# Writing the fp32 matmuls of a transform as four with 32 weight columns each

## The chip, the cores and the metric

The kernel runs on one core of one Trainium2 chip. The metric is the device time of one execution in microseconds (us). A core has five engines that run their own instruction lists side by side: TensorE (PE, with its weight loads PEld), VectorE (DVE), ScalarE (ACT), GpSimd (POOL) and SyncE (SP), which here issues most of the DMA transfers.

## What is computed

A two-dimensional Fourier transform of 2 x 3008 x 256 numbers, of which the real part is kept, and on its rows two feed-forward blocks:

```python
def _attn_ref(x):
    X = np.fft.fft(x, axis=1)
    X = np.fft.fft(X, axis=2)
    return X.real.astype(np.float32)

def _moe_ref(x, w_in, w_out):
    h = x @ w_in
    g = h * (1.0 / (1.0 + np.exp(-h)))
    return (g @ w_out).astype(np.float32)

def _moe2_ref(x, w_in, w_out):
    h = x @ w_in
    relu6 = np.clip(h + 3.0, 0.0, 6.0)
    g = h * relu6 / 6.0
    return (g @ w_out).astype(np.float32)
```

6016 rows pass through both blocks, with w_in of 256 x 2048 and w_out of 2048 x 256.

## The kernel before

The transform stands at the beginning, and the two blocks, which are most of the time, behind it. The sequence of 3008 is split as 47 x 64, and the transform has three steps on TensorE, all in fp32.

**First step.** x arrives in twelve chunks (`XCH`; seven for the first batch, five for the second, of one to four slots). `load_x` issues a chunk's DMAs; `fold` adds and subtracts its parts on VectorE (L339, L343, L344); `step1` multiplies the folded parts (128 weight columns each) with the table `t1_sb`, 96 columns, and ScalarE copies the result into `out1` (L370). The first of the two matmul rows of a chunk needs L343, the second L344. There are four big x buffers, so `load_x(i + 4)` stands behind `step1(i)`: the ninth chunk waits for the matmuls of the fifth, the tenth for those of the sixth, the twelfth for the eighth's. The SP queue issues the x loads in that order, then the first raw weights (L110).

**Second and third step.** `steps23(g)` runs for twelve groups g: it evacuates the group before last from PSUM into `eo` (ScalarE), multiplies `out1` with `t2_sb` (L393, 129 columns, and L394, 127), adds a term while copying to `o2` (ScalarE up to g = 7, then VectorE at L401), and multiplies the `o2` of the group before with `t3_sb` (L411, 128 columns). The first groups alternate with the last chunks of the first step.

**Fillers.** `busy` (L351) puts matmuls of a zero tile `nil` between the first chunks.

**psl.** `step1_last` (L379) has matmuls of another form, eight with 32 weight columns each, written to the four quarters of the 128 output partitions; 12 columns stream through.

**Behind it.** VectorE decodes the first block's weights, which come as 64-bit words, in the order in which the code calls `advance`: its first operations stand right behind the last fold. `split` makes a high and a low part of `eo` in a shorter format (`xhi` on ScalarE, `xlo` at L190 on VectorE). The first product of a block is `win1` (L303 to L305): three matmuls, high with high, low with high, high with low. It needs the decoded weights, `xhi` and `xlo`. Within each engine the order is that of the code.

An fp32 matmul leaves two records in the trace, each with a weight load: fp32 goes through the array in two passes.

Of the kernel before, what the change touches and what calls it, by code (L numbers as in the profile page):

```python
# [49 lines left out]
FF, P = 2048, 128  # L50
# [33 lines left out]
def body(tc, xh, x128, t1, t2, t3, w1, w128, w2, out):  # L84
    nc = tc.nc
    V, A, T, G = nc.vector, nc.scalar, nc.tensor, nc.gpsimd
# [225 lines left out]
    nil = fft.tile([P, P], F32, name="nil")  # L312
    w128_raw = fft.tile([P, NF, 2], U32, name="w128_raw")
    t1_sb = fft.tile([P, 6 * 104], F32, name="t1_sb")
    t2_sb = fft.tile([P, 272], F32, name="t2_sb")
# [19 lines left out]
    def fold(i):  # L335
# [8 lines left out]
            V.tensor_tensor(out=x[:, :, 384:512], in0=x[:, :, 0:128], in1=x[:, :, 128:256], op=ALU.subtract)  # L344
        return y

    def busy(times):

        ps = psA.tile([P, 512], F32, name="psw", tag="s3")
        for _ in range(times):  # L350
            T.matmul(ps[:, 0:128], nil, nil, start=True, stop=True)  # L351

    def step1(i, x):
        n, c, k = XCH[i]
        for h in range(2):
            ps = psX.tile([P, XB, 96], F32, name="ps1", tag=f"s{h}")
            src = x[:, :, 256 + 128 * h : 384 + 128 * h]
            if SLOTS[c] == 0:
                T.matmul(ps[:, 0, :], src[:, 0], t1_sb[:, 288 + 96 * h : 384 + 96 * h], start=True, stop=False)
                T.matmul(ps[:, 0, 0:48], src[:, 1], t1_sb[:, 480 + 48 * h : 528 + 48 * h], start=False, stop=True)  # L360
                k, j = 1, 0
            else:
                whole = UNFOLDED.get(i, 0)
                for m in range(whole):
                    T.matmul(ps[:, m, :], x[:, m, 0:128], t1_sb[:, 96 * h : 96 * h + 96], start=True, stop=False)
                    T.matmul(ps[:, m, :], x[:, m, 128:256], t1_sb[:, 192 * h : 192 * h + 96], start=False, stop=True)
                for m in range(whole, k):
                    T.matmul(ps[:, m, :], src[:, m], t1_sb[:, 96 * h : 96 * h + 96], start=True, stop=True)  # L368
                j = SLOTS[c]
            A.activation(  # L370
                out1[n][:, h, :, :, j : j + k], ps[:, :k, :].rearrange("p n (s q) -> p q s n", s=2), AF.Copy
            )
# [12 lines left out]

    def step2(g):
        n, t = divmod(g, 6)
        ps = psA.tile([P, 2, 256], F32, name="ps2", tag="s2")
        o2 = fft.tile([P, 2, 256], F32, name="o2", tag="o2", bufs=3)
        for i in range(2):  # L390
            q = 4 * (2 * t + i)
            e, o = (out1[n][:, h, q : q + 4].rearrange("p q s j -> p (q s j)") for h in range(2))
            T.matmul(ps[:, i, 0:129], e, t2_sb[:, 0:129], start=True, stop=True)  # L393
            T.matmul(ps[:, i, 129:256], o, t2_sb[:, 129:256], start=True, stop=True)  # L394

        x128 = xr[:, n, 2 * t : 2 * t + 2]
        if g < 8:
            for i in range(2):
                A.activation(o2[:, i, 0:129], ps[:, i, 0:129], AF.Identity, bias=x128[:, i : i + 1])
        else:  # L400
            V.tensor_tensor(  # L401
                out=o2[:, :, 0:129], in0=ps[:, :, 0:129], in1=x128.unsqueeze(2).to_broadcast([P, 2, 129]), op=ALU.add
            )
        A.activation(o2[:, :, 129:256], ps[:, :, 129:256], AF.Copy)
        return o2

    def step3(o2):
        ps = psA.tile([P, 2, 256], F32, name="ps3", tag="s3")
        for h in range(2):
            for i in range(2):  # L410
                T.matmul(  # L411
                    ps[:, h, 128 * i : 128 * i + 128], o2[:, i, 128 * h : 128 * h + 128], t3_sb,
                    start=True, stop=True,
                )
        return ps

    def evacuate(g, ps):
        n, t = divmod(g, 6)
        c = HALFB * n
        if t == 0:  # L420
            A.activation(eo[:, :, c : c + SELF], ps[:, :, 0:SELF], AF.Identity, scale=sign)
            A.activation(eo[:, :, c + SELF : c + SELF + 192], ps[:, :, 64:256], AF.Identity, scale=sign)
            return c + SELF + 192
        c += SELF - 64 + 256 * t
        A.activation(eo[:, :, c : c + 256], ps, AF.Identity, scale=sign)
        return c + 256
# [20 lines left out]
    o2, full, done = {}, {}, 0  # L447
    folded = fold(0)
    i = g = 0
    busy(8)  # L450

    def step1_next():

        nonlocal folded, i
        x = folded
        if i + 1 < nx:
            folded = fold(i + 1)
        step1(i, x)
        if 3 <= i < nx - 4:
            load_x(i + 4, nc.sync, nc.sync)  # L460
        if i + 4 == nx - 1:
            load_raw(1, w1, 0)
        i += 1
        if i == 1:
            nc.sync.dma_start(t2_sb[:, 0:257], t2)
            nc.sync.dma_start(t3_sb, t3)
            nc.sync.dma_start(xl, x128)
        if i < 3:
            busy(3 - i)
        if i == 4:  # L470
            nc.sync.dma_start(w128_raw, w128)
        if i == 5:
            G.tensor_tensor(out=xl[:, 0], in0=xl[:, 0], in1=xl[:, 1], op=ALU.add)
        if i == 7:
            step1_last()
        if i == nx - 4:
            load_raw(1, w1, 1)
            advance(steps, 1)

    def steps23(g):  # L480
        nonlocal done
        if 0 <= g - 2 < 12:
            done = evacuate(g - 2, full.pop(g - 2))
        if g < 12:
            o2[g] = step2(g)
        if 0 <= g - 1 < 12:
            full[g - 1] = step3(o2.pop(g - 1))

    while XCH[i][0] == 0:
        step1_next()  # L490
    while i < nx:
        steps23(g)
        g += 1
        step1_next()
        if i == nx - 2:
            begin(1, 0)
        elif i == nx - 1:
            advance(steps, 2600)
# [89 lines left out]
    while g < 14:  # L588
        if g < 12:
            steps23(g)  # L590
        if g in (7, 10):
            xs[(g - 6) // 3] = split_eo((g - 6) // 3, (g - 6) // 3)
        if g >= 11 and g - 11 < EARLY:
            win1_end(*units[g - 11])
        if g >= 10 and g - 10 < EARLY + AHEAD:
            win1(*units[g - 10])
        if g in (11, 12):
            steps23(g + 1)
            if g == 12:
                idle = psA.tile([P, 512], F32, name="psi", tag="s2")  # L600
            parts(*units[g - 11])
        if g >= 12:
            for _ in range(FILL):
                T.matmul(idle[:, 0:128], nil, nil, start=True, stop=True)
        if g in (9, 11):
            do_later()
        advance(steps, 1700 if g < 8 else (1400, 700, 1400, 0)[g - 10] if g > 9 else 1400)
        g += 1
# [140 lines left out]
    for i in range(n1):  # L749
# [13 lines left out]
        while saves:  # L763
            dst, src = saves.pop(0)
# [110 lines left out]
    for e, (k, f) in enumerate(units2):  # L875
# [30 lines left out]
        while late:  # L906
            dst, src, to = late.pop(0)
# [181 lines left out]
```

## Time and profile before

| | |
|---|---|
| median of 3 runs | 916.25 us (916.05 to 916.52) |
| the profiled execution, its own time | 916.08 us |
| its span | 914.0 us |
| TensorE busy | 908.0 us, 99% of the span |
| VectorE, ScalarE, GpSimd busy | 73%, 71%, 58% |
| last fp32 matmul ahead of the first product | about 44 us |

The span is the time from the first to the last instruction of the profiled execution. Busy shares are means over stages with different limits; for a change in the first 44 us the windows there matter. A wait is told with what ended it. Matmuls are pipelined and their ends are modelled, so their starts say more than their durations.

### The profile page before, as it was taken

Reading aid. Unit: us, or ns where it says so; the run is one execution under the profiler, and the core shown is the slowest. Engines: PE = TensorE matmul, PEld = TensorE weight load, DVE = VectorE, ACT = ScalarE, POOL = GpSimd, SP = SyncE. Lnnn points to the kernel's source line nnn. Section 1 sums busy time; section 2 is a strip of 40 time slices with the busy share of each in tenths; the row PEclk is TensorE's granted clock in tenths of the full one; section 3 lists DMA queues with packets and bytes.
Section 4 is the critical chain, followed back from the end, with each engine's and each line's share of the span. In section 5 each row is a group of like instructions: output and inputs, shape, how many; then the busy total and the mean of one; then the engine's idle time right before and its main releaser. Section 6 shows DMA issues by size and latency. Waiting matters only on the chain.

```text
span 914.0 us, 12150 instructions
## 1 busy us (share of the span) xinstructions
PE 908.0 (99%) x4286; PEld 774.4 (85%) x4286; DVE 664.1 (73%) x907; ACT 649.6 (71%) x1144; POOL 528.3 (58%) x391
## 2 busy tenths in 40 slices
PE   9999999999999999999999999999999999999998
PEld 8988888888888888888878888888888888888886
DVE  7989999989999999994664565565555555555544
ACT  4878777665766666677876677766776777677665
POOL 2065656655565656554675567755765675576553
PEclk9999999999999999999999999999999999999999
DMA  8564344034272726596330002020020002001001
GB/s 319 194 220 159 136 148 140 9 138 139 96 211 87 214 107 164 176 359 201 135 79 13 1 1 91 0 91 1 1 91 0 1 1 90 1 1 46 1 1 45
DMA packets 29768, 89.29 MB, mean 98 GB/s; under 512 B 2886, under 2 KB 16460, under 8 KB 27180
## 3 DMA queue, kind: packets, MB, share of 16 engines
q1 hardware_dynamic: 27692, 81.83, 25.5%
q0 software_dynamic: 1632, 6.16, 3.6%
q8 instruction: 33, 0.54, 0.2%
q10 hardware_dynamic: 384, 0.54, 0.2%
q14 instruction: 27, 0.22, 0.1%
HBM read 52.31 MB, written 36.20 MB: 97 GB/s over the span
## 4 chain that ended last, share of the span: by engine, by line
PE 98%; DVE 1%; DMA 0%; ACT 0%; issue 0%; SPq 0%
PE y L305 18%; PE y L303 18%; PE y L304 18%; PE ab L303 5%; PE ab L304 5%; PE ab L305 5%; PE pa L303 3%; PE pa L305 3%; PE pa L304 3%; PE pb L303 2%; PE pb L304 2%; PE pb L305 2%; PE ps L368 1%; PE ps L411 1%; PE pd L304 1%; PE pc L303 1%
## 5 line engine op out<-in xcount | busy, mean ns | idle before, releaser
L806 POOL TENSOR_TENSOR glo<-h,ghi 128x500 fp32r<-128x500 f32 (+1 forms) x191 | 247.0, 1306 | 180.9 <-ACT ghi L803 176.7
L624 POOL TENSOR_TENSOR glo<-h,ghi 128x500 fp32r<-128x500 f32 (+1 forms) x137 | 212.6, 1564 | 188.3 <-ACT h L582 176.1
L303 PE MATMUL y<-ghi,whi 128*128 128x500 f32 (+1 forms) x768 | 294.3, 383 | 0.0
L304 PE MATMUL y<-glo,whi 128*128 128x500 f32 (+1 forms) x768 | 294.3, 383 | 0.0
L305 PE MATMUL y<-ghi,wlo 128*128 128x500 f32 (+1 forms) x768 | 294.3, 383 | 0.0
L305 PEld LDWEIGHTS y<-ghi,wlo 128*128 128x128 f32 x768 | 144.2, 188 | 25.7
L303 PEld LDWEIGHTS y<-ghi,whi 128*128 128x128 f32 x768 | 144.2, 188 | 25.6
L304 PEld LDWEIGHTS y<-glo,whi 128*128 128x128 f32 x768 | 144.2, 188 | 25.6
L803 ACT ACTIVATE ghi<-h 128x500 fp32r<-128x500 f32 (+1 forms) x192 | 118.1, 625 | 48.3 <-DVE h L798 46.2
L581 ACT ACTIVATE ghi<-ab 128x500 fp32r<-128x500 f32 (+1 forms) x96 | 56.4, 588 | 85.3 <-DVE h L572 83.5
L798 DVE SCALAR_TENSOR_TENSOR h<-h,pc 128x500 f32<-128x500 f32 (+1 forms) x96 | 65.0, 677 | 71.2 <-ACT h L795 71.2
L928 DVE TENSOR_TENSOR pc<-u,pb 128x500 f32<-128x500 f32 (+1 forms) x48 | 32.9, 686 | 105.3 <-ACT u L864 105.3
L795 ACT ACTIVATE h<-pc,consts 128x500 f32<-128x500 f32 (+1 forms) x96 | 64.7, 674 | 40.1 <-DVE pc L928 38.2
L864 ACT ACTIVATE u<-pa 128x500 f32<-128x500 f32 (+1 forms) x96 | 56.7, 591 | 46.6 <-PE pa L305 43.4
L303 PE MATMUL ab<-xhi,whi 128*128 128x500 f32 (+1 forms) x192 | 74.2, 386 | 0.2 <-DVE st L561 0.2
L304 PE MATMUL ab<-xlo,whi 128*128 128x500 f32 (+1 forms) x192 | 73.8, 384 | 0.0
L305 PE MATMUL ab<-xhi,wlo 128*128 128x500 f32 (+1 forms) x192 | 73.6, 383 | 0.0
L561 DVE SCALAR_TENSOR_TENSOR st<-eb,w_sb,ab 128x500 f32<-128x500 f32 (+1 forms) x92 | 66.9, 727 | 6.4 <-PE ab L305 6.3
L572 DVE SCALAR_TENSOR_TENSOR h<-st,ab 128x500 f32<-128x500 f32 (+1 forms) x92 | 61.2, 665 | 6.1 <-PE ab L305 6.1
L795 ACT ACTIVATE h<-pd,consts 128x500 f32<-128x500 f32 (+1 forms) x96 | 64.8, 675 | 0.6 <-DVE pd L940 0.6
L798 DVE SCALAR_TENSOR_TENSOR h<-h,pd 128x500 f32<-128x500 f32 (+1 forms) x96 | 64.3, 670 | 1.2 <-ACT h L795 1.2
L582 ACT ACTIVATE h<-h 128x500 f32<-128x500 f32 (+1 forms) x96 | 60.0, 625 | 3.1
(165 smaller groups left out, 1574.6 us busy)
## 6 DMA issues: line engine op xcount, KB each, us to landing
raw<-in_w SPq DMA_DIRECT2D x16, 1024.0 KB, 6.9
y_d<-st SPq DMA_DIRECT2D x5, 1000.0 KB, 5.1
y_d<-st POOLq DMA_DIRECT2D x5, 1000.0 KB, 8.1
u<-y_d SPq DMA_DIRECT2D x5, 1000.0 KB, 5.4
out<-st SPq DMA_DIRECT2D x19, 250.0 KB, 2.2
w2h_d<-h SPq DMA_DIRECT2D x8, 512.0 KB, 2.6
w2l_d<-t SPq DMA_DIRECT2D x8, 512.0 KB, 3.3
whi<-w2h_d SPq DMA_DIRECT2D x8, 512.0 KB, 5.8
```

What stands on the lines that cost most here:

```text
L303: T.matmul(o, wh, xhi, start=first, stop=False, **group)
L304: T.matmul(o, wh, xlo, start=False, stop=False, **group)
L305: T.matmul(o, wl, xhi, start=False, stop=last, **group)
L561: V.scalar_tensor_tensor(out=z[:, :n], in0=eb[:, :n], scalar=w128_sb[:, f : f + 1], in1=ab[:, :n], op0=ALU.mult, op1=ALU.add)
L572: V.scalar_tensor_tensor(out=h[:, 0, :n], in0=z[:, :n], scalar=2.0, in1=ab[:, :n], op0=ALU.mult, op1=ALU.subtract)
L582: A.activation(h[:, s, :n], src, AF.Silu)
L624: eng.tensor_tensor(out=glo[:, s, :n], in0=h[:, s, :n], in1=ghi[:, s, :n], op=ALU.subtract)
L795: A.activation(h[:, i, :n], c[:, :n], AF.Relu, bias=three)
L798: V.scalar_tensor_tensor(out=h[:, i, :n], in0=h[:, i, :n], scalar=6.0, in1=c[:, :n], op0=ALU.min, op1=ALU.mult)
L803: A.activation(g[0][:, i, :n], h[:, i, :n], AF.Copy)
L806: E.tensor_tensor(out=g[1][:, i, :n], in0=h[:, i, :n], in1=g[0][:, i, :n], op=ALU.subtract)
L864: A.activation(t[:, :n], pa[:, :n], AF.Copy)
```

## The change

A helper `narrow` writes one matmul as four, each with 32 of the 128 weight columns, into the quarter of the output partitions that belongs to them. The moving columns are the same in all four. The fillers, the whole first step, the second step up to the ninth group (g < 9) and the third step that is issued up to then (eight groups) use it: 155 matmuls become 620. The rest of the kernel is as it was.

```diff
+    def narrow(o, wt, x, start=True, stop=True):
+        for c in range(0, P, 32):
+            T.matmul(o[c : c + 32], wt[:, c : c + 32], x, start=start, stop=stop)
+
     def busy(times):
 
         ps = psA.tile([P, 512], F32, name="psw", tag="s3")
         for _ in range(times):
-            T.matmul(ps[:, 0:128], nil, nil, start=True, stop=True)
+            narrow(ps[:, 0:128], nil, nil)
...
             if SLOTS[c] == 0:
-                T.matmul(ps[:, 0, :], src[:, 0], t1_sb[:, 288 + 96 * h : 384 + 96 * h], start=True, stop=False)
-                T.matmul(ps[:, 0, 0:48], src[:, 1], t1_sb[:, 480 + 48 * h : 528 + 48 * h], start=False, stop=True)
+                narrow(ps[:, 0, :], src[:, 0], t1_sb[:, 288 + 96 * h : 384 + 96 * h], start=True, stop=False)
+                narrow(ps[:, 0, 0:48], src[:, 1], t1_sb[:, 480 + 48 * h : 528 + 48 * h], start=False, stop=True)
...
                 for m in range(whole, k):
-                    T.matmul(ps[:, m, :], src[:, m], t1_sb[:, 96 * h : 96 * h + 96], start=True, stop=True)
+                    narrow(ps[:, m, :], src[:, m], t1_sb[:, 96 * h : 96 * h + 96], start=True, stop=True)
...
     def step2(g):
         n, t = divmod(g, 6)
+        mm = narrow if g < 9 else T.matmul
...
-            T.matmul(ps[:, i, 0:129], e, t2_sb[:, 0:129], start=True, stop=True)
-            T.matmul(ps[:, i, 129:256], o, t2_sb[:, 129:256], start=True, stop=True)
+            mm(ps[:, i, 0:129], e, t2_sb[:, 0:129], start=True, stop=True)
+            mm(ps[:, i, 129:256], o, t2_sb[:, 129:256], start=True, stop=True)
...
-    def step3(o2):
+    def step3(o2, mm):
...
         if 0 <= g - 1 < 12:
-            full[g - 1] = step3(o2.pop(g - 1))
+            full[g - 1] = step3(o2.pop(g - 1), narrow if g < 9 else T.matmul)
```

On TensorE, from the sixth chunk's matmuls (`ps` from `x`) up to `psl`, a row of the kernel before is one matmul, or several where an x and a number follow:

```order
L368 MATMUL ps_270<-t_sb,x_147 128x96 x4
L368 MATMUL ps_276<-t_sb,x_147 128x96 x4
L359 MATMUL ps_287<-t_sb,x_148 128x96
L360 MATMUL ps_287<-t_sb,x_148 128x48
L359 MATMUL ps_291<-t_sb,x_148 128x96
L360 MATMUL ps_291<-t_sb,x_148 128x48
L379 MATMUL psl<-t_sb,xl 32x12 x8
```

At the same place now, where the helper's line L349 stands for all of them:

```order
L349 MATMUL ps_393<-t_sb,x_147 32x96 x16
L349 MATMUL ps_411<-t_sb,x_147 32x96 x16
L349 MATMUL ps_434<-t_sb,x_148 32x96 x4
L349 MATMUL ps_434<-t_sb,x_148 32x48 x4
L349 MATMUL ps_444<-t_sb,x_148 32x96 x4
L349 MATMUL ps_444<-t_sb,x_148 32x48 x4
L383 MATMUL psl<-t_sb,xl 32x12 x8
```

Nothing moved against its neighbours; each matmul of 128 output partitions is four of 32 at its old place.

The narrow form ends on TensorE with the third step of the eighth group (`ps` from `o`, x16). What follows up to the first product reads in the changed kernel:

```order
L349 MATMUL ps_1006<-t_sb,o_940 32x128 x16
L398 MATMUL ps_1026<-t_sb,out_1_142 128x129
L399 MATMUL ps_1026<-t_sb,out_1_142 128x127
L398 MATMUL ps_1026<-t_sb,out_1_142 128x129
L399 MATMUL ps_1026<-t_sb,out_1_142 128x127
L416 MATMUL ps_1034<-t_sb,o_987 128x128 x4
...
L303 MATMUL ab<-xhi_977,whi_0_932 128x510
L304 MATMUL ab<-xlo_978,whi_0_932 128x510
```

From there on the rows are those of before, five lines further down in the code. On VectorE, ScalarE, GpSimd and SP every row stands where it stood.

## Rows read from the trace of the kernel before

**Rows 1.** The page: busy us (share, instructions) of each engine; the chain by engine

```profile
PE 908.0 (99%) x4286; PEld 774.4 (85%) x4286; DVE 664.1 (73%) x907; ACT 649.6 (71%) x1144; POOL 528.3 (58%) x391
PE 98%; DVE 1%; DMA 0%; ACT 0%; issue 0%; SPq 0%
```

**Rows 2.** Windows of 5 us: busy PE, PEld, DVE, ACT, POOL; clock, DMA share, GB/s

```profile
15.00:20.00 5.00, 5.00 (x60) 4.92 (x59) 3.57 (x6) 3.42 (x11) 0.00 (x0) 1.00 0.91 307
20.00:25.00 5.00, 5.00 (x48) 5.00 (x46) 4.22 (x7) 3.32 (x10) 0.00 (x0) 1.00 0.95 352
...
35.00:40.00 5.00, 5.00 (x48) 5.00 (x47) 4.79 (x7) 5.00 (x14) 0.00 (x0) 1.00 0.61 210
```

**Rows 3.** VectorE in order of time: start, us, what, [idle before <-what ended it]

```profile
13.62 0.68 DVE L344 TENSOR_TENSOR x<-x 128x512 f32<-128x512 f32 x1
...
19.01 1.22 DVE L339 TENSOR_TENSOR x<-x 128x1024 f32<-128x1024 f32 x1 [1.32 <-DMA x<-in_xh]
...
22.20 1.23 DVE L339 TENSOR_TENSOR x<-x 128x1024 f32<-128x1024 f32 x1 [0.64 <-DMA x<-in_xh]
...
37.89 1.23 DVE L160 TENSOR_TENSOR wlo<-lo,whi 128x1024 fp32r<-128x1024 f32 x1 [0.17 <-ACT whi L178]
...
42.70 1.21 DVE L190 TENSOR_TENSOR xlo<-eo,xhi 128x1020 fp32r<-128x1020 f32 x1
```

**Rows 4.** Waits of the first 44 us: us in total, times, longest

```profile
DVE x L339 <- DMA x<-in_xh: 3.9, 6, 1.3
```

**Rows 5.** TensorE in order of time, the first product

```profile
43.81 0.48 PE L303 MATMUL ab<-xhi,whi 128*128 128x510 f32 x1
```

**Rows 6.** TensorE in order of time, matmuls of 96, 129 and 127 columns

```profile
11.64 0.39 PE L365 MATMUL ps<-t_sb,x 128*128 128x96 f32 x2
11.86 0.39 PE L366 MATMUL ps<-t_sb,x 128*128 128x96 f32 x2
...
23.13 0.38 PE L394 MATMUL ps<-t_sb,out 128*128 128x127 f32 x2
23.35 0.39 PE L393 MATMUL ps<-t_sb,out 128*128 128x129 f32 x2
```

**Rows 7.** TensorE in order of time, eight records of 128 columns and what follows

```profile
20.19 1.06 PE L411 MATMUL ps<-t_sb,o 128*128 128x128 f32 x8
21.09 1.95 PE L368 MATMUL ps<-t_sb,x 128*128 128x96 f32 x16
```

**Rows 8.** TensorE in order of time, 96 and 48 columns in turn, then `psl`

```profile
15.74 0.39 PE L359 MATMUL ps<-t_sb,x 128*128 128x96 f32 x2
15.97 0.35 PE L360 MATMUL ps<-t_sb,x 128*128 128x48 f32 x2
16.15 0.43 PE L359 MATMUL ps<-t_sb,x 128*128 128x96 f32 x2
16.41 0.35 PE L360 MATMUL ps<-t_sb,x 128*128 128x48 f32 x2
16.69 0.32 PE L379 MATMUL psl<-t_sb,xl 128*32 128x12 f32 x16
...
L379 PE MATMUL psl<-t_sb,xl x16: 179/179/201, 16.7 to 16.8; 128*32 128x12 f32 x16
```

**Rows 9.** TensorE in order of time, the fifth and sixth chunk's last matmuls

```profile
13.42 2.48 PE L368 MATMUL ps<-t_sb,x 128*128 128x96 f32 x20
```

**Rows 10.** The SP queue in order of time: x loads, then raw weights

```profile
14.06 1.11 SPq L333 DMA_DIRECT2D x<-in_xh  x2
15.94 1.11 SPq L333 DMA_DIRECT2D x<-in_xh  x2
...
20.40 1.12 SPq L110 DMA_DIRECT2D raw<-in_w  x2
```

**Rows 11.** DMA queue q8: packets, MB, share; whole span, then 18 to 19.5 us

```profile
q8 instruction: 33, 0.54, 0.2%
q8 instruction: 1, 0.02, 3.8%
```

More of the change, by code (lines that the diff above doesn't have):

```diff
@@ L364, in step1 @@
                 for m in range(whole):
-                    T.matmul(ps[:, m, :], x[:, m, 0:128], t1_sb[:, 96 * h : 96 * h + 96], start=True, stop=False)
-                    T.matmul(ps[:, m, :], x[:, m, 128:256], t1_sb[:, 192 * h : 192 * h + 96], start=False, stop=True)
+                    narrow(ps[:, m, :], x[:, m, 0:128], t1_sb[:, 96 * h : 96 * h + 96], start=True, stop=False)
+                    narrow(ps[:, m, :], x[:, m, 128:256], t1_sb[:, 192 * h : 192 * h + 96], start=False, stop=True)
                 for m in range(whole, k):
-                    T.matmul(ps[:, m, :], src[:, m], t1_sb[:, 96 * h : 96 * h + 96], start=True, stop=True)
+                    narrow(ps[:, m, :], src[:, m], t1_sb[:, 96 * h : 96 * h + 96], start=True, stop=True)
                 j = SLOTS[c]
@@ L410, in step3 @@
             for i in range(2):
-                T.matmul(
+                mm(
                     ps[:, h, 128 * i : 128 * i + 128], o2[:, i, 128 * h : 128 * h + 128], t3_sb,
```

## The prediction

> **What bounds the kernel now.** I read the page's busy shares and chain first. TensorE is busy for 99% of the span, and the chain that ended last is 98% TensorE [rows 1]: over the whole run a nanosecond taken from TensorE should be a nanosecond of the span. But the change touches only the transform, so I then read windows of that stretch [rows 2]. From 15 to 25 and from 35 to 40 us TensorE has no gap; but VectorE is at 3.6 to 4.8 us of 5 and ScalarE at 5.00 of 5 between 35 and 40 us. So the question there is who is next, and how close.
>
> VectorE's own order answers it [rows 3]. Its waits in the first 44 us are for x chunks, 3.9 us in six pieces, the longest 1.3 us [rows 4]. The last two stand in front of the folds of the ninth and tenth chunk, at 19.01 us (1.32 us) and 22.20 us (0.64 us). From the tenth fold on VectorE runs nearly without a gap, through the folds and the decoding of the first weights, up to the `xlo` that ends at 43.91 us; its only other wait is 0.17 us for ScalarE. The first product, at 43.81 us on TensorE [rows 5], streams that `xlo` as its second matmul. So TensorE and VectorE arrive at 44 us together: the transform on TensorE may become much shorter, and the products start earlier only by as much as VectorE's chain moves. That chain hangs on the landing of x.
>
> **What one converted matmul costs.** An fp32 matmul leaves two records. With 128 weight columns the records start 0.11 us apart whether 96, 127, 128 or 129 columns stream: pairs are 0.22 to 0.23 us apart [rows 6], eight records of 128 columns take 0.90 us [rows 7]. So the stream does not set that; the weight load has the same pitch. The stream shows once: a 48-column pair starts 0.18 us before its successor where the 96-column pairs are 0.23 us apart, and the lost 0.04 us comes back behind it (0.26) [rows 8]. So 48 columns fewer are 0.04 us fewer, about 0.85 ns for a column of one pass. 96 columns stream in 82 ns, 128 in 109 ns, 129 in 110 ns.
>
> The kernel already has narrow matmuls: `psl`, 32 weight columns, 12 columns streamed, four quarters. Its 16 records take 0.32 us, of which the last one is 0.18 us [rows 8]: 0.14 us for 15 steps, 9 ns each, against 112 ns for a wide one. So the loads of four quarters overlap, and eight records (one old matmul) could issue in some 75 ns. What is left is the stream, two passes in each quarter, all quarters at once: 2 x 82 = 165 ns for 96 columns instead of 223, 2 x 41 = 82 for 48 columns, 2 x 110 = 220 for 127 to 129 columns.
>
> The bounds are far apart. The best is issue alone, 75 ns. The worst is that the streams of the quarters follow each other: 8 x 82 = 656 ns, 8 x 110 = 880 ns. Against the worst stands `psl` once more: sixteen streams of 12 x 0.85 = 10 ns would need 163 ns and took 140. I take 165 and 220 ns, since the quarters' loads there look fully independent.
>
> **The sum.** Converted are 11 fillers, 76 matmuls of the first step (72 with 96 columns, 4 with 48), 36 of the second step, 32 of the third: 155. On TensorE alone that is 72 x 58 + 4 x 141 + 68 x 3 ns = 4.2 + 0.6 + 0.2 = 5.0 us less work. The fillers wait for x anyway. Now what of it reaches 44 us:
>
> - The sixth chunk's eight matmuls run from 13.87 us (the last 16 of the 20 records at 13.42) to 15.66 us [rows 9]. VectorE's fold releases their second half at 14.30, so they would end near 15.1 us, 0.5 us sooner. Their end frees the buffer for the tenth chunk, whose DMAs SP issues at 15.94 us [rows 10]; VectorE waits for it until 22.20. The ninth chunk, issued at 14.06 us behind the fifth, has twelve matmuls in front: 0.7 to 0.8 us sooner.
> - Landing follows issue if the DMA engines have room. Between 15 and 20 us they move 307 GB/s, against 352 in the window behind it [rows 2], so I take the 0.5 us as landed.
> - So the fold at 22.20 starts 0.5 us sooner, VectorE's chain with it, and `xlo` too. ScalarE has to keep up: its first weight waits for the raw load issued at 20.40 us, behind the twelfth chunk, which waits for the eighth's matmuls; those end 0.9 us sooner. Then ScalarE is full but has 0.5 us less to wait.
> - TensorE gains another 1 to 1.5 us before 44 us, and stands waiting for `xlo` with it. From 44 us on nothing is changed, and everybody is 0.5 us earlier.
>
> Bounds for the 0.5: at most all VectorE's waits from 19 us on, 1.32 + 0.64 + 0.17 = 2.1 us; at least nothing, or below nothing by the rivals. The profiled execution took 916.08 us with a span of 914.0, 0.17 us under the median. 916.08 - 0.5 = 915.6, beside the median **915.8 us**.
>
> **Rivals.** *The whole wait goes.* If x lands as early as VectorE can take it (quarters that run at 75 ns free the buffers 1 to 1.7 us sooner), the chain gains 1.0 to 2.1 us: 914.2 to 915.2. Against it: DMA is at 0.91 to 0.95 of its time there [rows 2].
>
> *The instructions themselves (slower).* A converted matmul is 16 instructions with its loads instead of 4: 155 x 12 = 1860 more within 40 us. TensorE's instructions come by DMA, 33 packets of 0.54 MB in all, 16 KB each, and the one at 18 us took 3.8% of 16 engines for 1.5 us, 0.9 us of one engine [rows 11]. 1860 x 64 bytes are 7 such packets more, some four of them before 22 us. Every x load is spread over the engines and waits for its slowest: if the packets all fall to one engine that is already full, x is late by up to 4 x 0.9 us, less the 0.5: 3.1 us, 919.3. It decides from 0.5 us of such delay on; half of it is 917.5. For less of it speaks that the engines have 5 to 9% to spare there.
>
> [...]
>
> *Quarters in program order (slower).* The loop over quarters is outside, so a quarter's two passes follow each other, and need the same part of the array. If the engine kept strictly to that order, only the second pass of one quarter could overlap the first of the next: four streams to a matmul, 4 x 82 = 327 ns for 96 columns and 440 for 129. TensorE would have 72 x 0.10 + 68 x 0.21 - 0.2 = 21.6 us more, all on the path from 8 us on: 916.2 + 21.6, about 938. `psl` is written in that same order, and eight matmuls of it, each with a load of 32/128 x 112 = 28 ns between its passes, would take 224 ns, not 140. That speaks against it, for short streams.
>
> [...]
>
> *Partly shared streams.* If 129 columns cost 240 instead of 220 ns, the last two steps lose 1 us, which the 1 to 1.5 us in front of 44 us absorb: 915.8 to 917.
>
> **How the numbers follow.** The forecast (0 to 1 us less) has 0.58, the whole wait 0.12, partly shared streams 0.04, the instructions' own transfers 0.16, program order 0.10. Measurement can tell about 0.2%, 1.8 us, so "faster" means under 914.4: only the far end of the whole wait, 0.04. "Slower" means over 918.1: program order and half of the instruction case, 0.18. The rest, 0.78, is no change. A range from 914.4 to 918.2 leaves out program order, less than half of the instruction case and the end of the whole wait, together about 0.2.
>
> **What would show it.** Right: narrow records of 96 columns whose eight take about 0.165 us and those of 128 about 0.22; TensorE idle before the first product, waiting for `xlo`; VectorE's wait for the tenth chunk ending near 21.7 us; that product near 43.3 us. Wrong: eight records in 0.33 us or more (program order); longer waits of VectorE for x with more than one instruction packet before 20 us (instructions); a granted clock below 1.00 before 44 us, because shorter bursts leave TensorE idle between chunks.

## The result and the profile after

The changed kernel takes 925.0 us (median of 4 runs, 924.59 to 927.75), the kernel before beside it 916.4 us (4 runs, 916.05 to 916.92): a ratio of 1.0097, interval 1.0083 to 1.0112. That is 8.6 us slower, outside the range of the prediction (914.4 to 918.2). The profiled execution took 925.05 us with a span of 922.9 us, against 914.0.

The page of after (busy time, chain by engine) answers to [rows 1]; the instruction queue's line answers to the first of [rows 11]:

```profile
PE 907.6 (98%) x5216; PEld 771.7 (84%) x5216; DVE 664.7 (72%) x907; ACT 649.2 (70%) x1144; POOL 527.6 (57%) x391
PE 97%; issue 1%; DVE 1%; DMA 1%; ACT 0%; SPq 0%
q8 instruction: 41, 0.67, 0.3%
```

TensorE is as busy as before (907.6 us for 908.0), and the span is 8.9 us longer: it stands still somewhere. The page says little of where, only that "issue" (time in which an engine waits for nothing that the profile shows) is now 1% of the chain, and that eight instruction packets more come by. The windows say where (as in [rows 2]: busy PE, PEld, DVE, ACT, POOL; granted clock as a share of the full one, DMA share, GB/s):

```profile
15.00:20.00 5.00, 3.45 (x142) 2.98 (x142) 3.76 (x7) 1.44 (x6) 0.64 (x1) 1.00 0.89 285
20.00:25.00 5.00, 3.40 (x79) 3.33 (x83) 4.37 (x6) 1.72 (x6) 0.00 (x0) 0.71 0.74 259
25.00:30.00 5.00, 4.79 (x181) 4.58 (x173) 4.69 (x12) 3.35 (x10) 0.00 (x0) 0.95 0.86 321
30.00:35.00 5.00, 2.45 (x61) 2.45 (x64) 0.47 (x3) 0.49 (x1) 0.00 (x0) 0.74 0.43 172
35.00:40.00 5.00, 5.00 (x194) 5.00 (x188) 3.24 (x4) 4.78 (x11) 0.00 (x0) 0.92 0.02 3
```

From 30 to 35 us no engine does much: TensorE 2.45 us of 5, VectorE and ScalarE 0.5 us each, DMA 0.43. So for most of that time it is neither another engine's work nor a transfer of data that TensorE waits for. And the granted clock has fallen below 1.00 in windows where it was 1.00. TensorE in order of time (start, us, what, idle before and what ended it):

```profile
12.00 2.50 PE L349 MATMUL ps<-t_sb,x 128*32 128x96 f32 x108 [1.47 <-issue]
...
21.60 0.40 PE L349 MATMUL ps<-t_sb,out 128*32 128x127 f32 x2 [2.61 <-issue]
21.83 1.94 PE L349 MATMUL ps<-t_sb,x 128*32 128x96 f32 x48
23.47 2.00 PE L349 MATMUL ps<-t_sb,out 128*32 128x129 f32 x32
25.18 1.26 PE L349 MATMUL ps<-t_sb,o 128*32 128x128 f32 x32
26.23 1.53 PE L349 MATMUL ps<-t_sb,x 128*32 128x96 f32 x64
27.55 1.09 PE L349 MATMUL ps<-t_sb,out 128*32 128x129 f32 x32
28.43 1.08 PE L349 MATMUL ps<-t_sb,o 128*32 128x128 f32 x32
29.30 0.49 PE L349 MATMUL ps<-t_sb,x 128*32 128x96 f32 x10
32.55 2.30 PE L349 MATMUL ps<-t_sb,x 128*32 128x96 f32 x51 [2.75 <-issue]
...
44.59 0.95 PE L349 MATMUL ps<-t_sb,o 128*32 128x128 f32 x25 [0.65 <-issue]
...
52.79 0.48 PE L303 MATMUL ab<-xhi,whi 128*128 128x510 f32 x1
```

**The streams are as forecast.** 64 records of 96 columns (eight old matmuls) start at 26.23 and the next group at 27.55: 0.165 us for each old matmul. 32 records of 128 columns (four old ones) start at 28.43 and the next group at 29.30: 0.87 us, 0.22 each. The four quarters do run at once.

**TensorE waits for its own instructions.** The idle pieces are "issue". From 21.60 to the next piece at 32.55 there are 252 records, each with a weight load, so about 504 instructions: two blocks of 256. A block fills one packet: 0.67 MB in 41 packets are 16 KB each, and the burst below shows one packet for each 256 instructions. The packets of the instruction queue in the trace start late, too: one flies from 19.24 to 20.19 us and TensorE goes on at 21.60, the next but one from 30.14 to 31.02 and TensorE goes on at 32.55: 1.4 to 1.5 us after the landing each time. Between them the second block is entered at about 26.5 us (128 records after 21.60, counted off the rows) and the block behind it runs at 32.55: some 6 us. The waits summed up (us in total, times, longest):

```profile
PE ps L349 <- issue: 8.3, 6, 2.8
```

**And it pays twice.** About the end of the two long pieces the granted clock falls to 0.50 (22.1 to 25.5 and 32.4 to 35.8 us): the 32 records of 129 columns at 23.47 need 1.71 us to the next group, those at 27.55, at a granted clock of 1.00, 0.88. Against the same groups at 1.00, the first stretch costs 1.7 us and the second 1.5, an estimate of 3.2 us from these rows.

The path to the end went through ScalarE, then VectorE (the first fence has rows of ScalarE, the second those of VectorE that answer to [rows 3]):

```profile
33.77 0.49 ACT L374 ACTIVATE out<-ps 128x384 f32<-128x384 f32 x1 [4.00 <-PE ps L349]
35.05 0.49 ACT L374 ACTIVATE out<-ps 128x384 f32<-128x384 f32 x1 [0.79 <-PE ps L349]
35.44 1.18 ACT L116 ACTIVATE lo<-raw 128x1024 f32<-128x1024 f32 x1
```

```profile
20.35 1.22 DVE L339 TENSOR_TENSOR x<-x 128x1024 f32<-128x1024 f32 x1 [1.34 <-DMA x<-in_xh]
...
23.05 1.23 DVE L339 TENSOR_TENSOR x<-x 128x1024 f32<-128x1024 f32 x1
...
36.66 0.70 DVE L122 TENSOR_SCALAR lo<-lo 128x1024 f32<-128x1024 f32 x1 [6.12 <-ACT lo L116]
...
46.23 1.23 DVE L160 TENSOR_TENSOR wlo<-lo,whi 128x1024 fp32r<-128x1024 f32 x1 [1.43 <-ACT whi L178]
```

The folds of the ninth and tenth chunk are 1.3 and 0.9 us late, not 0.5 early. Then ScalarE's first work on the raw weights (L116) stands in its list behind the copying of results (L374) of matmuls that TensorE has no instructions for; VectorE waits 6.12 us for it. L116 starts at 35.44 us for 27.56 before (+7.9), the first product at 52.79 for 43.81 [rows 5] (+9.0), which is the whole loss.

### The profile page after: what moved, and what is told of

Its sections match the earlier page's. It is cut to its first block, busy times and chain, and to the rows that moved or that the text cites. A ratio compares the mean times of both kernels' runs of the same rounds, so it can differ in the third digit from the quotient of the medians.

```text
span 922.9 us, 14010 instructions
## 1 busy us (share of the span) xinstructions
PE 907.6 (98%) x5216; PEld 771.7 (84%) x5216; DVE 664.7 (72%) x907; ACT 649.2 (70%) x1144; POOL 527.6 (57%) x391
## 4 chain that ended last, share of the span: by engine, by line
PE 97%; issue 1%; DVE 1%; DMA 1%; ACT 0%; SPq 0%
PE y L303 18%; PE y L304 18%; PE y L305 18%; PE ab L303 5%; PE ab L304 5%; PE ab L305 4%; PE ps L349 3%; PE pa L303 3%; PE pa L304 3%; PE pa L305 3%; PE pb L303 2%; PE pb L304 2%; PE pb L305 2%; PE pd L304 1%; PE pc L303 1%
```

## The experiments

All are compared with the kernel before at 916.3 to 916.4 us, run beside them. The first two do one half of the change each, without the fillers; `narrow` is the loop over the four quarters. In the cuts of code, `...` and the notes behind `#` stand for what is left out. Times inside the transform come from one profiled execution of each kernel, and two traces of the same code differ there: the burst below has the code of before up to 50 us, and groups 5 to 8 up to about 32 us; the tenth chunk's fold starts at 22.20 us in before, 22.00 in the burst and 21.62 in groups 5 to 8, and L116 at 27.56, 28.10 and 27.77. Less than 0.6 us there tells nothing by itself.

**First step only.**

```
-   T.matmul(ps[:, m, :], src[:, m], t1_sb[...], ...)
+   narrow(ps[:, m, :], src[:, m], t1_sb[...], ...)        # and the other first-step matmuls
    step2, step3: T.matmul as before
```

> Narrow matmuls in the first step alone (76 of the 155); fillers, second and third step as before. Theory (instruction supply: two pages of 256 instructions, the next one comes some 4 us after a page is entered, later under DMA load): idle time of TensorE that nothing in the profile releases, in pieces that end about 1.4 us behind the landing of an instruction packet, 2 to 5 us in all, since eight narrow and eight wide matmuls in turn use 160 instructions in 3.1 us; time 917.5 to 920.5. Rival A (x late because instruction packets share a DMA engine with it): no such idle time, but longer waits of VectorE for x; 916.5 to 919. Rival B (the first step's own gain outweighs it): 915.5 to 916.2.

922.2 us (ratio 1.0059, interval 1.0045 to 1.0073). The first-step half alone loses 5.8 of the 8.6 us, more than expected (917.5 to 920.5). The cause has the same face, in the waits of TensorE's first 55 us, and the granted clock is 0.5 here too, from 27.1 to 30.5 us, after the longest of them:

```profile
PE ps L349 <- issue: 5.2, 3, 2.1
```

The first product on TensorE, for 43.81 before:

```profile
49.55 0.48 PE L303 MATMUL ab<-xhi,whi 128*128 128x510 f32 x1
```

So the half that was to bring the gain (96 columns) does most of the harm: it uses up instructions fastest (256 in 16 x 0.165 = 2.6 us), in the place where x flies.

**Second and third step only.**

```
    step1: T.matmul as before
+   mm = narrow if g < 9 else T.matmul      # step2; step3 likewise
```

> Narrow matmuls in the second and third step alone (68 of the 155), where the stream leaves nothing to gain. Theory (instruction supply): up to the last chunk a page of 256 lasts some 5.7 us, which covers most fetches; behind it 16 narrow matmuls last 3.5 us and a fetch about 4, so some 0.5 us of idle time a page for three or four pages; 917 to 919, with the granted clock at 1.00 throughout because no gap is long. Rival (narrow streams themselves are slower for 128 columns): longer spacing of the records without idle time. Rival (only long gaps with the clock drop cost time): 916.2 to 916.6.

917.8 us (1.0017, 1.0008 to 1.0026): the expected number, but not the expected way. Three or four idle pieces of 0.5 us were expected; TensorE has one on issue. In the profiled execution (918.6 us, the slowest of ten) 2.2 us are missing at the first product, and 1.8 of them are there already when ScalarE gets the raw weights (ScalarE, then TensorE):

```profile
29.33 1.14 ACT L116 ACTIVATE lo<-raw 128x1024 f32<-128x1024 f32 x1 [1.40 <-DMA raw<-in_w]
...
41.80 0.64 PE L349 MATMUL ps<-t_sb,o 128*32 128x128 f32 x15 [0.84 <-issue]
...
45.97 0.48 PE L303 MATMUL ab<-xhi,whi 128*128 128x510 f32 x1
```

That is a second loss: the load came late, 29.33 for 27.56 us.

**Halves.** Two of 64 weight columns, everywhere that the change has four of 32: a third of the added instructions (620 of 1860; the expectation has a half).

```
-   for c in range(0, P, 32): T.matmul(o[c : c + 32], wt[:, c : c + 32], x, ...)
+   for c in range(0, P, 64): T.matmul(o[c : c + 64], wt[:, c : c + 64], x, ...)
```

> All 155 matmuls written as two with 64 weight columns in place of four with 32: half of the added instructions. Theory (instruction supply): a page lasts 32 x 0.165 = 5.3 us with 96 columns, 7 us with 128, longer than an undisturbed fetch of 4 us; at most 2 us of idle time under DMA load; 915.5 to 918, records of 96 columns still 0.165 us a matmul. Rival (clock or array form, not the number of instructions): as slow as the change, 923 to 926.

917.2 us (1.0007, 0.9998 to 1.0016), inside the expected range: no change that can be told. No idle piece on issue, clock 1.0 throughout the transform, and 96 columns take 0.165 us here too (32 records to the next group in 1.32 us). The tenth fold starts at 21.87, not earlier than in groups 5 to 8; the first product is 0.5 us later than before, and the raw weights are 1.1 us later (TensorE, then ScalarE, then TensorE, which waits for ScalarE behind it):

```profile
24.43 1.52 PE L349 MATMUL ps<-t_sb,x 128*64 128x96 f32 x32
25.75 1.07 PE L349 MATMUL ps<-t_sb,out 128*64 128x129 f32 x16
...
28.67 1.16 ACT L116 ACTIVATE lo<-raw 128x1024 f32<-128x1024 f32 x1 [2.20 <-DMA raw<-in_w]
...
30.71 1.18 PE L349 MATMUL ps<-t_sb,o 128*64 128x128 f32 x16 [0.82 <-ACT o L404]
```

**Quarters in the fifth and sixth chunk only**, where the prediction put its gain.

```
+   mm = narrow if i in (4, 5) else T.matmul      # in step1
```

> Narrow matmuls for the fifth and sixth chunk alone (20 matmuls), those that free the buffers of the ninth and tenth chunk; all else as before. Theory (instruction supply was the only fault; the predicted gain is there): their instructions fit into the two pages that are loaded by then, no idle time without a releaser, the ninth and tenth chunk's DMAs issue 0.5 to 0.8 us sooner, VectorE's wait at the tenth chunk shrinks and the first product starts about 0.5 us sooner: 0.3 to 0.9 us less than the kernel before. Rival (x is bound by the DMA engines, not by when it is issued): no change within 0.2 us. Rival (instruction pages already cost here): 0.5 to 2 us more.

918.0 us (1.0021, 1.0011 to 1.0030): a miss. I had counted the 240 instructions as too few to reach a block's end early; the end was reached inside the sixth chunk. And the packet (14.69 to 15.66 us) went out among the x loads (TensorE, then the eighth chunk's fold on VectorE, which had no wait before):

```profile
16.91 0.27 PE L349 MATMUL ps<-t_sb,x 128*32 128x96 f32 x1 [1.37 <-issue]
...
17.85 0.96 DVE L339 TENSOR_TENSOR x<-x 128x768 f32<-128x768 f32 x1 [2.05 <-DMA x<-in_xh]
```

**Sixth chunk only, and halves in the fifth and sixth.** Two smaller doses.

```
+   mm = narrow if i == 5 else T.matmul           # 32 columns
```

> Quarters in the sixth chunk only: 96 instructions more than before, in one place, everything else as before. Theory (TensorE is handed its instructions in blocks of 256 and waits where a block is not there yet): the block of the sixth chunk's end is entered at about the time of before, so no idle time on issue; TensorE is through the chunk about 0.35 us sooner (8 matmuls fewer nanoseconds each, as the 96-column ones took 0.165 for 0.22 us), and of that at most 0.3 us reaches the first product: 915.8 to 916.6 us, same. Rival (the split costs time by itself, wherever it stands): idle time on issue again, as after the fifth and sixth chunk together, 917.5 to 918.5 us.

```
+   mm = narrow if i in (4, 5) else T.matmul      # narrow with 64 columns
```

> Two matmuls of 64 columns each in the fifth and sixth chunk only, 80 instructions more. Theory: the block's end is not reached sooner than it is handed over, so no idle time on issue; the two chunks take about 0.5 us less of TensorE, the tenth chunk's buffer comes free sooner, and the first product by 0 to 0.5 us: 915.8 to 916.4 us. Rival (any earlier entry of a block costs an x load): as with the quarters in these chunks, 917 to 918.5 us.

917.4 us (1.0010, 1.0001 to 1.0019) and 917.1 us (1.0006, 0.9997 to 1.0015). Both lie above what was expected (915.8 to 916.6 and 915.8 to 916.4 us); the halves' time is the one that the rival named, 917 to 918.5, though by the interval it cannot be told from no change. TensorE is not short of instructions in either (at most 0.2 us on issue), and neither got the gain: the first product is at 45.23 and 44.52 us. In the first fence VectorE in the kernel with the sixth chunk, in the second VectorE and ScalarE in the one with the halves:

```profile
20.42 1.23 DVE L339 TENSOR_TENSOR x<-x 128x1024 f32<-128x1024 f32 x1 [2.25 <-PE ps L400]
```

```profile
21.54 1.22 DVE L339 TENSOR_TENSOR x<-x 128x1024 f32<-128x1024 f32 x1
...
28.90 1.13 ACT L116 ACTIVATE lo<-raw 128x1024 f32<-128x1024 f32 x1 [1.07 <-DMA raw<-in_w]
```

The first row names TensorE as what ended the wait, but a fold of the ninth chunk does not need that matmul. The trace's landing events show what it was: of the 16 landings of that chunk's second load, 15 were there by 19.36 us and the last at 20.29; before, all 16 were there by 18.89. The packet flew 0.45 us sooner than before (17.80 for 18.25 us). That alone does not decide: in groups 5 to 8 a packet flies from 17.81 us too, and that load's 16 landings are there by 18.41. In the halves the tenth fold is 0.66 us sooner than before (and 0.08 sooner than in groups 5 to 8); the raw weights are 1.3 us later.

**Fillers only.** More instructions, without touching any work that something waits for.

```
-   T.matmul(ps[:, 0:128], nil, nil, start=True, stop=True)
+   narrow(ps[:, 0:128], nil, nil)
```

> Only the eleven filler matmuls ahead of the transform's waits are written as four: 132 instructions more, none of them work that anything waits for. Theory (an instruction packet of 16 KB that flies among the x loads makes one of the 16 landings of a chunk late): the first block is entered earlier, its packet leaves at about 9 to 11 us in place of the time of before, and folds of VectorE wait for x by 0.5 to 2 us more: 916.6 to 918.5 us. Rival (packets cost only the starved engine): no chunk lands later, 916.2 to 916.5 us.

917.8 us (1.0018, 1.0009 to 1.0027), as the theory had it: TensorE has no idle time on issue, but the first packet leaves at 10.46 us in place of 18.25, the sixth chunk's fold waits 1.06 us for x (none before), and the raw weights come 2.6 us later:

```profile
13.12 1.23 DVE L339 TENSOR_TENSOR x<-x 128x1024 f32<-128x1024 f32 x1 [1.06 <-DMA x<-in_xh]
...
30.21 1.16 ACT L116 ACTIVATE lo<-raw 128x1024 f32<-128x1024 f32 x1 [1.73 <-DMA raw<-in_w]
```

**Groups 5 to 8 only** (counted from 0; the third step issued with them is that of groups 4 to 7). Four times the instructions of the sixth chunk, behind the landing of x and of the first raw weights.

```
+   mm = narrow if 4 < g < 9 else T.matmul      # step2; step3 likewise
```

> Quarters in the second and third step of the groups 5 to 8 only, on TensorE from 32.7 to 39.9 us of before, behind the landing of the last x and of the first raw weights: 384 instructions more, four times those of the sixth chunk (96, 1.0 us more) and three times those of the fillers (132, 1.4 us more). Theory (an early packet costs because the x and raw loads that fly then are late by it; TensorE itself waits only where a block of 256 is used up in under about 4 us): folds and the raw landing as before, at most one idle piece on issue of under 1 us about 38 to 41 us: 916.2 to 917.3 us. Rival (the time goes with the number of instructions added): 3 to 5 us more, 919.5 to 921.5 us.

916.6 us (1.0002, 0.9993 to 1.0011), as the theory had it. TensorE runs the narrow groups one behind the other without an idle piece, and the first product is where it was:

```profile
37.88 1.06 PE L349 MATMUL ps<-t_sb,out 128*32 128x129 f32 x32
38.76 1.07 PE L349 MATMUL ps<-t_sb,o 128*32 128x128 f32 x32
...
43.72 0.48 PE L303 MATMUL ab<-xhi,whi 128*128 128x510 f32 x1
```

So the number of instructions does not set the cost (384 more here for 0.1 us, 96 more in the sixth chunk for 1.0); when their packets fly and how fast a block is used up goes with it. 256 narrow instructions are 16 old matmuls: here, with 127 to 129 columns, 3.5 us. Two such blocks ran without a wait here; the longer run of them in the second and third step has the one wait of 0.84 us.

**A burst of 256 narrow matmuls in a quiet place.** The kernel before with 1024 instructions more, whose results nobody uses, behind the transform (two runs).

```
+   for m in range(256):
+       c = 32 * (m % 4)
+       T.matmul(idle[c : c + 32, 128:140], nil[:, c : c + 32], nil[:, 0:12], start=True, stop=True)
```

> The kernel before, with 256 matmuls of 32 weight columns and 12 moving columns added behind the transform, at about 50 us, where neither x nor weights are short: 1024 instructions more, results not used. By the columns they move they take under 5 us. Theory (blocks of 256 instructions, about 4 us from the entry of one to the start of the next): four blocks, TensorE idle on issue for about 3 us in each, 14 to 18 us more, 930 to 935 us. [...]

933.5 us (1.0184, 1.0165 to 1.0203): 17.1 us more, as the theory had it. 8.2 us are idle on issue, less than the 12 of the theory; for much of the rest TensorE works at a granted clock of 0.50. TensorE in order of time, then one window (columns as above):

```profile
50.92 1.97 PE L603 MATMUL psi<-nil 128*32 128x12 f32 x162
53.12 0.50 PE L603 MATMUL psi<-nil 128*32 128x12 f32 x30 [0.24 <-issue]
57.66 1.90 PE L603 MATMUL psi<-nil 128*32 128x12 f32 x128 [4.03 <-issue]
61.39 1.90 PE L603 MATMUL psi<-nil 128*32 128x12 f32 x128 [1.83 <-issue]
65.39 1.05 PE L603 MATMUL psi<-nil 128*32 128x12 f32 x64 [2.10 <-issue]
```

```profile
60.00:65.00 5.00, 1.90 (x128) 1.80 (x128) 0.00 (x0) 0.00 (x0) 0.00 (x0) 0.50 0.01 3
```

Exactly 128 records and 128 weight loads, 256 instructions, then nothing, with DMA at 0.01 of its time. The blocks start 3.7 and 4.0 us apart. Within one: a block is entered at 57.66, the packet of the next flies from 59.01 to 60.05, TensorE goes on with it at 61.39; so 1.35 us until the packet moves, 1.0 in flight, 1.35 until it runs. For the next block these are 1.7, 0.9 and 1.3. The granted clock falls to 0.5 here too, at 55.8 us, within the 4 us without work, and is back at 1.00 at 69.4 us.

The kernels side by side. "Packets" are those of the instruction queue between 5 and 27 us; the last column is the median against that of before in the same comparison. The last but one counts the first product from the start of the fifth chunk's fold (9.69 to 10.28 us), which takes out by how much a whole trace is early or late; the burst, with the code of before up to there, has 33.95 us:

| kernel | instructions added | packets | first raw work (L116) | first product | the same, from the fifth chunk's fold | median |
|---|---|---|---|---|---|---|
| before | | 1 | 27.56 us | 43.81 us | 33.99 us | |
| groups 5 to 8 | 384 | 1 | 27.77 | 43.72 | 34.03 | +0.1 us |
| halves, chunks 5 and 6 | 80 | 2 | 28.90 | 44.52 | 34.50 | +0.7 |
| halves everywhere | 620 | 3 | 28.67 | 44.32 | 34.40 | +0.8 |
| sixth chunk | 96 | 2 | 28.45 | 45.23 | 35.32 | +1.0 |
| fillers | 132 | 2 | 30.21 | 45.84 | 35.79 | +1.4 |
| second, third step | 816 | 2 | 29.33 | 45.97 | 35.99 | +1.4 |
| chunks 5 and 6 | 240 | 2 | 29.32 | 45.47 | 35.54 | +1.7 |
| first step | 912 | 3 | 32.93 | 49.55 | 39.59 | +5.8 |
| after | 1860 | 4 | 35.44 | 52.79 | 42.64 | +8.6 |

Every kernel with a second packet among the x and raw loads begins on its raw weights 0.9 us later or more; groups 5 to 8, without one, begins 0.2 us later, whatever it added, and the burst, which up to there is the kernel before, 0.5. Only "first step" and "after", where TensorE stands on issue for 5.2 and 8.3 us, lose more than 2 us. None of these kernels beats the one before.

What goes with a late load shows in its 16 landings. In before, the burst and groups 5 to 8 the 16th is at most 0.5 us behind the 15th in all x loads issued from 5 us on and in the first raw load. In each of the other eight kernels of the table at least one of these loads has a 16th landing 0.8 to 2.1 us behind its 15th. In seven of them a packet has landed 1.1 to 3.3 us before that landing; in the eighth, second and third step, the 16th landing of a load is 1.0 us behind at 24.28 us already, before the packet leaves at 24.49, and the reason for that is not shown. The fillers show it most plainly: with the packet from 10.46 to 11.40 us, three loads have 15 landings by 11.83, 12.50 and 12.84 us and the 16th at 13.00, 13.66 and 13.99 (before: 0.01 us behind); with the packet from 24.95 to 25.92 the first raw load has 15 by 28.79 and the last at 30.18 (before: 27.52 and 27.54).

## Why the prediction was wrong

**The price of a narrow matmul was right**: 0.165 us for 96 columns and 0.22 for 128, as forecast. It bears out the 0.85 ns for a column of one pass (0.165 us for 2 x 96 columns), which the prediction had from a single pair of rows. The rival of quarters in program order is false; the sum printed for its cost comes to 21.3 us, not 21.6, which changes nothing. Four quarters take 0.165 us, the two streams of 82 ns that the prediction put for quarters that overlap wholly, and the trace of after has records that start out of the order of the list, in which all of `psl` stands behind the matmuls of 48 columns (17.29 us for a record of `psl`, 17.32 for one of 48 columns).

```profile
17.29 0.18 PE L383 MATMUL psl<-t_sb,xl 128*32 128x12 f32 x1
17.32 0.21 PE L349 MATMUL ps<-t_sb,x 128*32 128x48 f32 x1
```

**The step that failed is the price of the instructions.** The prediction had the right count (1860 more, 16 KB packets) and made a rival of them, but priced them only as DMA time, at most 3.1 us through late x. Its 64 bytes for an instruction agree with the pages: 0.54 MB for the 2 x 4286 instructions of before are 63 bytes each, 0.67 MB for the 2 x 5216 of after 64. For TensorE's own wait for them its sum has no term, and no row showed that there is none. The packets of before could have given the doubt: they start 10 us apart or more, so no row showed how fast they can come. The runs show some 4 us for a block of 256 when nothing else flies, and some 6 among the loads of after, where 256 narrow instructions of 96 columns are used up in 16 x 0.165 = 2.6 us. In after TensorE waits 8.3 us on issue. Added up by the rows to ScalarE's first raw work, which is 7.9 us late: TensorE comes to the first group of the second step 1.0 us late (17.91 for 16.94), the two long idle pieces are 5.4 and the stretches at a clock of 0.50 3.2, and the groups in which TensorE is faster give some 1.5 back, some 8 us together. How much the clock alone would cost, without the starving, no run separates.

How many instructions TensorE has at hand, the burst bounds: 128 records and 128 loads stand between two pieces, and 1024 instructions already bring three pieces of 1.8 to 4.0 us, which looks like two blocks of 256, one in use and one on its way. That reading fits the rows; no run tests it against another small depth.

**The instructions' own transfers**: that they cost something was right, and the size fair. Where TensorE was not short of instructions, extra packets go with 1.4 us (fillers) and 1.0 (sixth chunk), and with 0.7 and 0.8 in the halves, which are not clear of nothing by their intervals; all lie inside the 0 to 3.1 us that were allowed. That a packet among loads goes with one late landing of a load's 16 is what the landings above show, in seven kernels of eight; which DMA engine carries a packet the trace does not tell, nor why the same packet at 17.8 us did no harm in groups 5 to 8.

**The 0.5 us through the tenth chunk's buffer** came as far as the issue of the load when nothing starved. Counted from the fifth chunk's fold, the tenth chunk's first DMA is issued after 6.1 us in before, the burst and groups 5 to 8, and after 5.7 in the sixth chunk and both halves: 0.4 us sooner. That the landing follows the issue, which the prediction took as given, is not shown: counted in the same way, the tenth fold comes after 11.7 to 12.4 us in the first three kernels, after 11.5 and 11.9 in the halves and after 13.0 in the sixth chunk. And nothing arrived at the first product. In both halves the eighth chunk's 16th landing came 1.2 and 1.0 us behind its 15th, its fold 1.2 to 1.3 us later than in before, and so the first raw load was issued 0.4 and 0.7 us later and landed 1.1 and 1.3 us later. The prediction named that load and dismissed it with the eighth chunk's earlier end, which became a later one.

**The bound at 44 us** was read rightly for the kernel before, but a bound holds only as long as the others keep up: in after, VectorE waits 6.1 us for ScalarE and ScalarE for TensorE. The clock below 1.00 stood among the signs of being wrong, though because of shorter bursts; here the 0.50 stands about the end of idle pieces of 2.6 and 2.8 us on issue.

## What to carry to other kernels

Splitting a matmul multiplies instructions (1860 more for 155 matmuls here); count how long a block of 256 of them lasts. Here TensorE waited on issue where a block lasted 2.6 us, once for 0.84 us where it lasted 3.5, and a new block took 3.7 to 4.0 us even with idle DMA; so by these runs a wait is to be looked for below some 4 us, however well the streams overlap. Behind the longest waits here (2.1, 2.6, 2.8 and 4.0 us) the granted clock was also 0.50 for a while (3.4 us, and 13.6 in the burst). Instruction packets can fly among the loads, and the kernels with a second one there begin on the raw weights 0.9 us later or more: look where they fly, and keep added instructions out of stretches where a late landing is on the path. A wait of type "issue" that is near zero in a profile does not say that there is room: it was 0% of the chain in before, and TensorE waits 8.3 us on it in after.

## What the runs showed of the hardware that was not expected

- TensorE, where it waits for instructions, goes on 1.25 to 1.55 us after a packet has landed, and a packet takes 0.9 to 1.5 us (0.88 to 1.51 over the 41 of after). With the 1.35 to 1.7 us before it flies in the burst, that is 3.7 to 4.0 us from block to block with idle DMA.
- Sixteen narrow fp32 instructions run in 0.165 us (96 columns), 10 ns each, so a block lasts 2.6 us: TensorE can use instructions faster than they come (a block in 3.7 to 4.0 us in the burst).
- Halves do what quarters do: two of 64 weight columns also take 0.165 us for 96 columns, with half the instructions.
- In seven kernels an instruction packet among loads goes with one of a load's 16 landings being 0.8 to 2.1 us behind the other 15; in the sixth-chunk run a fold came 1.4 us later with that landing.
